# Kernel gradients of two output tiles per PSUM bank, written dense by ScalarE and permuted for the DRAM layout by GpSimd

## The chip, the cores and the metric

The kernel runs on one core of one Trainium2 chip. The metric is the device time of one execution in microseconds (us); a kernel is judged by the median of its runs. The core has five engines that run side by side, each through its own queue in a fixed order: TensorE (PE in the profile; its weight loads are PEld), VectorE (DVE), ScalarE (ACT), GpSimd (POOL) and SyncE (SP). Results of matmuls land in PSUM, which has banks of 512 fp32 columns; everything else on the chip is in SBUF, with 128 partitions.

## The reference

The reference is the forward pass and all gradients of one block, with L = 2048 positions, D = 576 channels, N = 128 states per channel and F = 4608 hidden units:

```python
xn = layernorm(x)
K  = einsum("dn,dnl,dn->dl", C, exp(dt*A*l), dt*B).real   # one kernel per channel
s  = irfft(rfft(xn) * rfft(K))[:L] + xn * Dskip           # long convolution
g  = silu((silu(xn @ w1) * (xn @ w3)) @ w2)               # gated FFN
out = x + s * g
# returned: out and the gradients of x, A, B, C (re, im), log_dt, Dskip, w1, w3, w2
```

What the change touches is the gradient of the convolution kernel, gK[d, l]: the correlation of the gradient of `s` with `xn`, for each channel. Two things are wanted of it downstream: gK itself and gK times the position l. Both are contracted with the state exponentials to give the gradients of A, B, C and log_dt.

## The kernel before

The program is built by a tile framework that schedules it: each piece of code gets a due time with `self.at(us)`, and the framework writes one fixed order of instructions per engine from those due times, with semaphore waits between engines. Nothing is reordered at run time. Independent work is mixed by choosing due times that overlap.

The stages, by the time in the profile: a prologue (layernorm, DFT matrices), the generation of K beside the first FFN matmuls, the forward convolution beside the second FFN matmul, then the backward part, which has two streams on the same engines:

- **FFN backward** (`phase6_group`, 18 groups of 256 hidden units). Per group: loads `w2r`, `h_n` and `gg_n` on GpSimd's queue (L1139, L1144, L1145), activations on ScalarE (L1149, L1151), matmuls into `ph` (L1172), ScalarE's copy to `gh` (L1175), VectorE's products (L1178), then weight gradients into `pgw` (L1200, L1218), which ScalarE copies to `gw` (L1204, L1221) and GpSimd's queue stores (L1205, L1222). The ring of `gw` has four buffers of each kind.
- **Convolution backward** (`ssm_bwd_conv`, `conv_bwd_quarter`, four quarters of 144 channels each). The sequence is cut into four blocks of 512, and the correlation is done by spectra of these blocks (DFT as matmul).

In one quarter, first the spectra `g` of the gradient are made (L564, copied out by ScalarE at L568). Then, for the blocks i = 3, 2, 1, 0 of gK, VectorE forms the spectrum Z as a sum of 4 - i complex products (`cmul_acc`, L601 to L610) and from it ZZ (L913 or L916, then L918). PE transforms ZZ back in four tiles of 128 positions x 144 channels (`idft_tile`, eight matmuls of 144 columns each, L582). This is one burst. Each tile has a PSUM bank of its own from a pool of three (`et_ps`). ScalarE empties it with four ACTIVATEs of 72 columns (L926, L927): for each half h of the channels one scaled by 1/512 and one scaled by the position (`lcol`). They write the order that DRAM is to have: in `gk_st` the tile's index t runs fastest, so that neighbouring elements of one ACTIVATE lie 32 elements apart in the buffer. After block 0 two DMAs on SyncE's queue store `gk_st` to `gK_dram` (L929). The second half of the quarter makes the gradient of `xn` in the same way, with VectorE adding each tile to `gx` (L947).

After the four quarters the parameter stage runs (`param_quarter`): it loads `gz` from `gK_dram` (L959, from 1317.9 us on), multiplies with the state exponentials on PE (L970) and reduces on VectorE (L977, L979), beside the last FFN groups. The last stage, `phase6_inputs`, makes the gradient of x (`px`, L1262) from the stored FFN gradients, which are loaded with transposing DMAs from SyncE's queue (L1123).

Of the kernel before, what the change touches and what calls it, by code (L numbers as in the profile page):

```python
# [10 lines left out]
ACT = mybir.ActivationFunctionType  # L11
# [3 lines left out]
BF16 = mybir.dt.bfloat16  # L15
I32 = mybir.dt.int32
P = 128
# [43 lines left out]
class K:  # L61
# [777 lines left out]
    def ssm_bwd_conv(self, T0, TQ, ps):  # L839
        nc, cfg = self.nc, self.cfg  # L840
        D, LT = cfg.D, cfg.LT
        self.gK_dram = self.dram.tile([4, P // 2, D // 64, 2, 2, 16 * LT], BF16, name="gK_dram")
        with self.tc.tile_pool(name="b_k", bufs=1, side="right") as kp, self.tc.tile_pool(name="b_z", bufs=2, side="right") as zp:
            self.at(T0)
            self.lcol = kp.tile([P, LT], FP32, name="lcol")
            nc.vector.tensor_scalar(out=self.lcol[:], in0=self.irow[:, 0:LT], scalar1=float(P),
                                    scalar2=self.pcol[:, 0:1], op0=ALU.mult, op1=ALU.add)
            nc.vector.tensor_scalar(out=self.lcol[:], in0=self.lcol[:], scalar1=1.0 / 512, scalar2=None, op0=ALU.mult)
            self.ones_col = kp.tile([P, 1], BF16, name="ones_col")
            nc.vector.memset(self.ones_col[:], 1.0)  # L850
            for g in range(4):
                self.conv_bwd_quarter(g, kp, zp, ps, T0 + g * TQ, TQ)

    def ssm_bwd_params(self, T0, TC, S_all, ps):
        cfg = self.cfg
# [7 lines left out]
            for g in range(4):  # L863
                self.param_quarter(g, gz, S_all, qp, ps, T0 + TC * g * D // 64, TC)

    def conv_bwd_quarter(self, g, kp, zp, ps, T0, TQ):
        nc, cfg = self.nc, self.cfg
        D, LT, KT, NB = cfg.D, cfg.LT, cfg.KT, cfg.NB
        W = D // 4
        cs = slice(g * W, (g + 1) * W)  # L870
        A2 = [None] * NB
        Az = [None] * NB
        fl = lambda t_: t_[:].rearrange("p q r k d -> p (q r) (k d)")
        self.at(T0)
        gs = kp.tile([P, LT, W], BF16, name="gs")
        nc.sync.dma_start(out=gs[:], in_=self.GS_dram[g])
        for b in range(NB):
            a3 = kp.tile([P, 3, KT, W], BF16, name=f"a3_{b}")
            nc.sync.dma_start(out=a3[:, 1], in_=self.UH_dram[g, b, :, 0])
            nc.sync.dma_start(out=a3[:, 0], in_=self.UH_dram[g, b, :, 1])  # L880
            A2[b], Az[b] = a3[:, None, 1:3], a3[:, None, 0]
            self.spectrum_variants(A2[b], Az[b])
        G = []
        for b in range(NB):
            self.at(T0 + TQ * 0.05 * b)
            G.append(kp.tile([P, 1, 2, KT, W], BF16, name=f"g_{b}"))
            self.dft_block(ps, lambda tt: gs[:, b * KT + tt, :], G[b])
        gds = ps.tile([P, 512], FP32, name="et_ps")
        for b in range(NB):
            prod = zp.tile([P, KT, W], BF16, name="gsxn")  # L890
            for tt in range(KT):
                t = b * KT + tt
                nc.vector.tensor_tensor(out=prod[:, tt, :].rearrange("p (h d) -> p h d", h=2),
                                        in0=gs[:, t, :].rearrange("p (h d) -> p h d", h=2),
                                        in1=self.nat4(self.xn_bf[:, t, :])[:, g], op=ALU.mult)
            for tt in range(KT):
                nc.tensor.matmul(gds[0:1, 0:W], lhsT=self.ones_col[:], rhs=prod[:, tt, :], start=(b == 0 and tt == 0),
                                 stop=(b == NB - 1 and tt == KT - 1))
        gds_sb = zp.tile([1, W], BF16, name="gds_sb")
        nc.scalar.copy(out=gds_sb[:], in_=gds[0:1, 0:W])  # L900
        with nc.allow_non_contiguous_dma(reason="small vector store"):
            nc.sync.dma_start(out=self.aps["out_9"].rearrange("(o h g d) -> o g h d", o=1, h=2, g=4)[:, g],
                              in_=gds_sb[:].rearrange("p (h d) -> p h d", h=2))
        st = kp.tile([P, D // 64, 2, 8, 2, LT], BF16, name="gk_st")
        nxt = None
        for i in range(NB - 1, -1, -1):
            self.at(T0 + TQ * (0.2 + 0.1 * (NB - 1 - i)))
            Z = zp.tile([P, 1, 2, KT, W], BF16, name="Z")
            for k, m in enumerate(range(i, NB)):
                self.cmul_acc(Z, A2[m - i], Az[m - i], G[m], zp, k == 0, True)  # L910
            ZZ = zp.tile([P, 1, 2, KT, W], BF16, name="ZZ")
            if nxt is not None:
                nc.vector.scalar_tensor_tensor(out=fl(ZZ), in0=fl(nxt), scalar=self.sgn[:, 0:1], in1=fl(Z), op0=ALU.mult,  # L913
                                               op1=ALU.add)
            else:
                nc.vector.tensor_copy(out=ZZ[:], in_=Z[:])  # L916
            nxt = Z
            nc.vector.tensor_scalar(out=ZZ[:, 0, :, 0, :], in0=ZZ[:, 0, :, 0, :], scalar1=self.hrow[:, 0:1], scalar2=None,  # L918
                                    op0=ALU.mult)
            for oc in range(KT):  # L920
                t = i * KT + oc
                pt = ps.tile([P, 512], FP32, name="et_ps")
                self.idft_tile(pt, ZZ, oc)
                for h in range(2):
                    pv = pt[:, h * W // 2:(h + 1) * W // 2].rearrange("p (c d) -> p c d", d=8)
                    nc.scalar.activation(out=st[:, :, 0, :, h, t], in_=pv, func=ACT.Copy, scale=1.0 / 512)  # L926
                    nc.scalar.activation(out=st[:, :, 1, :, h, t], in_=pv, func=ACT.Copy, scale=self.lcol[:, t:t + 1])  # L927
        for hf in range(2):
            nc.sync.dma_start(out=self.gK_dram[g, :, :, :, hf, :],  # L929
                              in_=st[64 * hf:64 * hf + 64].rearrange("p c k d h t -> p c k (d h t)"))  # L930
        for b in range(NB):
            a3 = kp.tile([P, 3, KT, W], BF16, name=f"a3_{b}")
            nc.sync.dma_start(out=a3[:], in_=self.KH_dram[g, b])
            A2[b], Az[b] = a3[:, None, 1:3], a3[:, None, 0]
        for j in range(NB):
            self.at(T0 + TQ * (0.6 + 0.1 * j))
            Z = zp.tile([P, 1, 2, KT, W], BF16, name="Z")
            for k, i in enumerate(range(NB - j)):
                self.cmul_acc(Z, A2[i], Az[i], G[i + j], zp, k == 0, True)
            gx = zp.tile([P, KT, W], FP32, name="gx")  # L940
            nc.vector.tensor_tensor(out=gx[:], in0=gs[:, j * KT:(j + 1) * KT, :],
                                    in1=self.dskip_row[:, None, cs].to_broadcast([P, KT, W]), op=ALU.mult)
            for oc in range(KT):
                t = j * KT + oc
                pt = ps.tile([P, 512], FP32, name="et_ps")
                self.idft_tile(pt, Z, oc)
                nc.vector.tensor_tensor(out=gx[:, oc, :], in0=pt[:, 0:W], in1=gx[:, oc, :], op=ALU.add)  # L947
            nc.scalar.dma_start(out=self.GXN_dram[:, j * KT:(j + 1) * KT, cs], in_=gx[:])
# [439 lines left out]
```

## Time and profile before

| | |
|---|---|
| median of 13 runs | 2046.72 us (2031.19 to 2065.65) |
| the profiled execution | 2057.42 us, of which the span is 2055.6 us |
| granted TensorE clock, mean | 0.948 |
| PE busy | 1770.4 us, 86% of the span |
| DVE busy | 1428.6 us, 69% |
| ACT busy | 992.4 us, 48% |
| POOL busy | 365.8 us, 18% |
| L926 and L927 in the window 850 to 1290 us | 79.7 and 82.4 us busy, 128 instructions each |
| first and last of them | 857.1 and 1273.3 us |

The span is the time from the first to the last instruction of the profile. "Busy" counts a stretch once, however many instructions of an engine overlap in it; instructions on ACT and DVE do overlap, since one starts before the last one's end. A line such as `L926 ACT ACTIVATE gk_st<-et_ps` names the source line, the engine, the operation, and what it writes and reads; the shapes are partitions x elements per partition. A line of the waits says who waited for whom, the total in us, how often, and the longest. In a timeline a bracket at the end gives the idle time of the engine before that instruction and what ended it.

### The profile page before, as it was taken

What the parts mean: (1) busy time and instruction counts of PE and PEld (TensorE: products, weight loads), DVE (VectorE), ACT (ScalarE), POOL (GpSimd) and SP (SyncE); (2) the same over time, 40 slices, a digit from 0 to 9 for tenths busy, and PEclk for the clock granted to TensorE, in tenths of its full rate; (3) what the DMA queues carried; (4) which work ended last, traced back from release to release, by engine and by line L of the source; (5) the groups of instructions that cost most, each with busy time, mean ns of one, the idle gap of its engine ahead of it and who ended that gap; (6) DMA issues with size and microseconds to landing.
All of it is one profiled execution on the core that took longest, in us unless ns stands there. A gap on an engine that the chain in (4) does not pass through costs nothing. (4 is left out here: it accounts for less than half of the span.)

```text
span 2055.6 us, 42197 instructions
## 1 busy us (share of the span) xinstructions
PE 1770.4 (86%) x17174; PEld 1296.6 (63%) x17174; DVE 1428.6 (69%) x2772; ACT 992.4 (48%) x1668; POOL 365.8 (18%) x540
## 2 busy tenths in 40 slices
PE   2889999999699995899888998898899839999891
PEld 1544444444488874788767777786788727777681
DVE  7538888888387723595964958676788725858567
ACT  2778888888445545766636556343364200000000
POOL 4003333333312102111111211221112100000000
PEclk9899999999899997999999999999999969999996
DMA  3588888896966568365653645798899599999980
GB/s 83 195 285 307 305 296 301 290 321 248 303 145 168 133 139 268 124 197 153 171 162 100 200 149 163 200 264 203 184 223 215 158 225 215 193 233 191 212 154 22
DMA packets 595505, 416.06 MB, mean 202 GB/s; under 512 B 404912, under 2 KB 537136, under 8 KB 590704
## 3 DMA queue, kind: packets, MB, share of 16 engines
q1 hardware_dynamic: 539632, 264.00, 53.8%
q0 software_dynamic: 30544, 120.94, 17.1%
q10 hardware_dynamic: 25136, 28.44, 5.3%
q8 instruction: 134, 2.20, 0.5%
q14 instruction: 59, 0.48, 0.1%
HBM read 133.01 MB, written 188.01 MB: 156 GB/s over the span
## 5 line engine op out<-in xcount | busy, mean ns | idle before, releaser
L719 PE MATMUL pgu<-wmB_w,xnT 128*128 128x512 bf16 x1152 | 282.4, 380 | 1.8 <-ACT E_k L392 1.4
L1262 PE MATMUL px<-wTB_w,guc 128*128 128x288 bf16 x1152 | 244.6, 293 | 26.3 <-DMA guc<-GU_dram 14.3
L1262 PE MATMUL px<-wTB_w,ggc 128*128 128x288 bf16 x1152 | 246.5, 293 | 21.7 <-DMA ggc<-GG_dram 12.0
L1218 PEld LDWEIGHTS <-xn_bf 128*128 128x128 bf16 x2304 | 227.3, 99 | 54.4 <-issue 25.2
L977 DVE TENSOR_TENSOR pr_q<-et_ps,pz 128x512 f32<-128x512 f32 x288 | 186.6, 681 | 93.5 <-PE et_ps L970 93.5
L1172 PE MATMUL ph<-w2T,goT 128*128 128x256 bf16 x1440 | 188.6, 282 | 7.9 <-ACT gh L1175 5.9
L719 PEld LDWEIGHTS <-xnT 128*128 128x128 bf16 x1152 | 103.2, 98 | 124.4 <-issue 19.5
L1279 ACT ACTIVATE t<-gx 128x576 f32<-128x576 f32 x16 | 10.9, 683 | 348.2 <-DVE gx L1265 304.2
L979 DVE TENSOR_REDUCE S_all<-pr_q 128x16 f32<-128x1024 f32 x144 | 174.0, 1212 | 0.5
L1200 PE MATMUL pgw<-go_o,h_n 128*128 128x288 bf16 x1152 | 158.8, 291 | 8.3 <-DVE h_n L1154 8.1
L1172 PEld LDWEIGHTS <-goT 128*128 128x128 bf16 x1440 | 141.7, 101 | 31.3 <-issue 7.6
L1221 ACT CAST gw<-pgw 128x256 bf16<-128x256 f32 x144 | 53.7, 379 | 219.3 <-PE pgw L1218 175.0
L1262 PEld LDWEIGHTS <-guc 128*128 128x128 bf16 x1152 | 114.5, 100 | 59.0 <-DMA guc<-GU_dram 15.9
L1218 PE MATMUL pgw<-gg_n,xn_bf 128*128 128x256 bf16 x1152 | 134.9, 279 | 17.7 <-ACT gw L1221 17.7
L784 PE MATMUL po<-w2g,hc 128*128 128x288 bf16 x1152 | 148.6, 286 | 1.7 <-DMA hc<-H_dram 1.7
L1262 PEld LDWEIGHTS <-ggc 128*128 128x128 bf16 x1152 | 114.0, 100 | 52.5 <-issue 11.4
L1200 PEld LDWEIGHTS <-h_n 128*128 128x128 bf16 x1152 | 113.1, 100 | 38.1 <-DVE h_n L1154 8.8
L1218 PE MATMUL pgw<-gu_n,xn_bf 128*128 128x256 bf16 x1152 | 132.2, 272 | 4.1 <-ACT gw L1221 2.0
L784 PEld LDWEIGHTS <-hc 128*128 128x128 bf16 x1152 | 111.3, 98 | 29.1 <-DMA hc<-H_dram 2.2
L722 ACT ACTIVATE s_t<-pgu 128x512 bf16<-128x512 f32 x144 | 87.4, 609 | 53.5 <-PE pgu L721 53.2
L1222 POOL DMA_DIRECT2D out_dram<-gw x144 | 77.6, 540 | 190.3 <-ACT gw L1221 186.1
L1175 ACT CAST gh<-ph 128x512 bf16<-128x512 f32 x144 | 83.3, 615 | 50.1 <-PE ph L1172 29.3
(305 smaller groups left out, 3724.9 us busy)
## 6 DMA issues: line engine op xcount, KB each, us to landing
GI_dram<-gu_t POOLq DMA_DIRECT2D x72, 512.0 KB, 5.7
H_dram<-h_t SPq DMA_DIRECT2D x72, 256.0 KB, 5.2
Q_dram<-q_k SPq DMA_DIRECT2D x36, 512.0 KB, 5.2
gg_n<-GI_dram POOLq DMA_DIRECT2D x18, 1024.0 KB, 5.6
h_n<-GI_dram POOLq DMA_DIRECT2D x18, 1024.0 KB, 8.7
GU_dram<-gu_n SPq DMA_DIRECT2D x36, 512.0 KB, 4.6
GG_dram<-gg_n SPq DMA_DIRECT2D x36, 512.0 KB, 7.1
E_dram<-E_k SPq DMA_DIRECT2D x18, 768.0 KB, 3.6
```

What stands on the lines that cost most here:

```text
L719: nc.tensor.matmul(pgu[:, j], lhsT=xnT[:, c, ts], rhs=wm[w][:, c, :], start=(c == 0), stop=False)
L722: nc.scalar.activation(out=s_t[:, :, q, :], in_=pgu[:, 0].rearrange("p (g f) -> p g f", g=ng), func=ACT.Silu)
L784: nc.tensor.matmul(pos[k][:, pi_, 0:pw], lhsT=hcs[k][:, fi, :], rhs=w2[fi][:, po:po + pw], start=(fi == 0), stop=(fi == FT - 1))
L977: nc.vector.tensor_tensor(out=pr[:, r], in0=T[r][:], in1=pz[:, s + r, h * 8:h * 8 + 8, :][:, :, None, :] .to_broadcast([P, 8, 2, AV]), op= ...
L979: nc.vector.tensor_reduce(out=S_all[:, 2 * s:2 * s + 2, d0:d0 + 8].rearrange("p k d -> p d k"), in_=pr[:].rearrange("p r d k a -> p d k r ...
L1172: nc.tensor.matmul(ph[j][:, k, :].rearrange("p (a f) -> p a f", f=P), lhsT=lw, rhs=rh, start=(n == 0), stop=(n == nfull))
L1175: nc.scalar.copy(out=gh[:, j], in_=ph[j][:])
L1200: nc.tensor.matmul(pgw[pi_][:, 0:pw], lhsT=hn[:, tt, fl * P:(fl + 1) * P], rhs=go_o[:, tt, po:po + pw], start=(tt == 0), stop=(tt == LT - 1))
L1218: nc.tensor.matmul(pw_[:, 0:FG], lhsT=self.xn_bf[:, tt, c * P:(c + 1) * P], rhs=nat[:, tt, :], start=(tt == 0), stop=(tt == LT - 1))
L1221: nc.scalar.copy(out=gw[:], in_=pw_[:, 0:FG])
L1222: nc.gpsimd.dma_start(out=aps[oname][c * P:(c + 1) * P, fb:fb + FG], in_=gw[:])
L1262: nc.tensor.matmul(px[pi_][:, 0:pw], lhsT=act[:, fi, :], rhs=wT[part][ai][:, f, po:po + pw], start=(fi == 0 and ai == 0), stop=(fi == FT - ...
```

## The change

The two tiles of a pair are transformed into one bank, side by side. ScalarE empties the pair with three ACTIVATEs that write dense rows of a new buffer `gk_sd` (two in rotation, one per block i): one of 288 columns for the scale 1/512, and one of 144 columns per tile for the position. When the four tiles of a block are in `gk_sd`, GpSimd copies them to `gk_st` in the order that DRAM is to have, with four copies of 288 elements per partition (9 x 8 x 4; one per scale k and half h); each writes runs of four elements and reads with a step of 288 elements. The two stores to `gK_dram` are as before and wait for GpSimd's copies now.

```diff
+                self.tc.tile_pool(name="b_s", bufs=2, side="right") as sp:
...
-            for oc in range(KT):
-                t = i * KT + oc
+            sd = sp.tile([P, KT, 2, W], BF16, name="gk_sd")
+            for o2 in range(0, KT, 2):
+                t = i * KT + o2
                 pt = ps.tile([P, 512], FP32, name="et_ps")
-                self.idft_tile(pt, ZZ, oc)
+                for j in range(2):
+                    self.idft_tile(pt[:, j * W:(j + 1) * W], ZZ, o2 + j)
+                nc.scalar.activation(out=sd[:, o2:o2 + 2, 0, :], in_=pt[:, 0:2 * W].rearrange("p (t d) -> p t d", t=2),
+                                     func=ACT.Copy, scale=1.0 / 512)
+                for j in range(2):
+                    nc.scalar.activation(out=sd[:, o2 + j, 1, :], in_=pt[:, j * W:(j + 1) * W], func=ACT.Copy,
+                                         scale=self.lcol[:, t + j:t + j + 1])
+            for k in range(2):
                 for h in range(2):
-                    pv = pt[:, h * W // 2:(h + 1) * W // 2].rearrange("p (c d) -> p c d", d=8)
-                    nc.scalar.activation(out=st[:, :, 0, :, h, t], in_=pv, func=ACT.Copy, scale=1.0 / 512)
-                    nc.scalar.activation(out=st[:, :, 1, :, h, t], in_=pv, func=ACT.Copy, scale=self.lcol[:, t:t + 1])
+                    nc.gpsimd.tensor_copy(out=st[:, :, k, :, h, i * KT:(i + 1) * KT],
+                                          in_=sd[:, :, k, h * W // 2:(h + 1) * W // 2].rearrange(
+                                              "p t (c d) -> p c d t", d=8))
```

Per quarter ScalarE goes from 64 ACTIVATEs of 72 columns to 24 (8 of 288 columns, 16 of 144), and GpSimd gains 16 copies. Matmuls and DMAs are the same in number and size.

More of the change, by code (lines that the diff above doesn't have):

```diff
@@ L842, in ssm_bwd_conv @@
         self.gK_dram = self.dram.tile([4, P // 2, D // 64, 2, 2, 16 * LT], BF16, name="gK_dram")
-        with self.tc.tile_pool(name="b_k", bufs=1, side="right") as kp, self.tc.tile_pool(name="b_z", bufs=2, side="right") as zp:
+        with self.tc.tile_pool(name="b_k", bufs=1, side="right") as kp, \
+                self.tc.tile_pool(name="b_z", bufs=2, side="right") as zp, \
+                self.tc.tile_pool(name="b_s", bufs=2, side="right") as sp:
             self.at(T0)
@@ L851, in ssm_bwd_conv @@
             for g in range(4):
-                self.conv_bwd_quarter(g, kp, zp, ps, T0 + g * TQ, TQ)
+                self.conv_bwd_quarter(g, kp, zp, sp, ps, T0 + g * TQ, TQ)
     def ssm_bwd_params(self, T0, TC, S_all, ps):
@@ L864, in ssm_bwd_params, with conv_bwd_quarter @@
                 self.param_quarter(g, gz, S_all, qp, ps, T0 + TC * g * D // 64, TC)
-    def conv_bwd_quarter(self, g, kp, zp, ps, T0, TQ):
+    def conv_bwd_quarter(self, g, kp, zp, sp, ps, T0, TQ):
         nc, cfg = self.nc, self.cfg
```

## Prediction

> **What bounds the kernel now.** I read the page first (span, busy shares), then the chain that ended last, then the waits and windows of the stretch that the diff touches. Times are of the profiled execution: 2057.42 us, of which the span is 2055.6. The 13 runs shown have a median of 2046.72, 0.5% lower. I work out a difference against the profiled execution and take it off the median.
>
> The page: TensorE (PE) is the fullest engine, and the changed work (L926, L927) lies between 857 and 1274 us. The chain, three pieces of it:
>
> ```profile
> 1623.29 10.64 PE pgw L1218 x96
> 1637.08 6.52 DMA out_dram<-gw
> 1643.67 4.87 SPq L1123
> ```
>
> The end is tied to the last FFN gradient group: its last gradient is stored at 1637, then SyncE issues transposed loads, then `px` runs to the end. PE takes its work in one written order. So what PE loses or gains between 857 and 1274 moves everything behind it by that much, as long as nothing else holds PE there. Next the waits of PE and VectorE (DVE) in that stretch (columns: total us, times, longest):
>
> ```profile
> PE et_ps L582 <- ACT gk_st L927: 22.4, 22, 3.2
> PE et_ps L582 <- DVE gx L947: 9.0, 3, 4.2
> PE ph L1172 <- ACT gh L1175: 5.3, 6, 1.3
> DVE gu_n L1178 <- ACT gh L1175: 40.1, 15, 5.4
> ```
>
> PE waits 22.4 us for a PSUM bank that ScalarE (ACT) has not yet emptied into `gk_st`. The wait for `gh` is partly the same thing: the `gh` copies are queued on ACT behind the `gk_st` burst. But DVE is nearly full in the same places. Windows around the four bursts (us of PE, PEld, DVE, ACT, POOL busy):
>
> ```profile
> 855.00:875.00 20.00, 15.38 (x147) 12.57 (x145) 16.50 (x29) 19.97 (x46) 0.56 (x1) 0.91 0.22 64
> 875.00:905.00 30.00, 27.00 (x282) 23.61 (x280) 28.78 (x51) 16.55 (x47) 8.09 (x15) 1.00 0.64 212
> 960.00:1013.00 53.00, 45.19 (x448) 37.54 (x447) 48.79 (x91) 36.00 (x97) 8.62 (x16) 0.97 0.42 123
> 1112.00:1160.00 48.00, 40.50 (x413) 35.05 (x411) 42.23 (x75) 32.62 (x88) 8.64 (x16) 0.96 0.51 157
> 1226.00:1275.00 49.00, 40.60 (x411) 34.92 (x410) 42.03 (x75) 31.85 (x88) 8.65 (x16) 0.97 0.42 132
> ```
>
> Over these 200 us PE is idle 31.3 (20-15.4, 30-27, 53-45.2, 48-40.5, 49-40.6), DVE 21.7. Both are late because of ACT, and DVE, which makes each ZZ, is the next limit.
>
> **The change, part by part.**
>
> *ACT.* A tile costs four scattered ACTIVATEs, 256 in all. They start 0.32 us apart:
>
> ```profile
> 861.26 0.80 ACT L926 ACTIVATE gk_st<-et_ps 128x72 bf16<-128x72 f32 x1
> 861.58 0.81 ACT L927 ACTIVATE gk_st<-et_ps,lcol 128x72 bf16<-128x72 f32 x1
> 960.28 0.62 ACT L568 CAST g<-et_ps 128x144 bf16<-128x144 f32 x3
> 974.63 0.70 ACT L1204 CAST gw<-pgw 128x288 bf16<-128x288 f32 x2 [0.52 <-PE pgw L1200]
> ```
>
> Two tiles are 8 x 0.32 = 2.56 us. After: one dense op of 288 columns (0.70 / 2 = 0.35) and two of 144 (0.62 / 3 = 0.21 each), 0.77 us. Over 32 pairs ACT sheds 32 x 1.79 = 57 us. PE needs about 0.06 us per matmul of 144 columns, 1.0 us for the 16 of a pair, so ACT keeps ahead with three banks: the 22.4 us wait goes. One price: reading starts after two tiles, not one, so 0.5 us later per burst, which a burst that is some 1.8 us x 2 shorter covers.
>
> *PE.* The built program has the same matmuls in nearly the same order; a few FFN matmuls that stood between two tiles of a pair now stand behind it. I put that at nothing, since they stay within the burst.
>
> *GpSimd (POOL).* 64 copies of 288 elements per partition, four per block row. No row shows this copy (it reads with a step of 576 bytes). The rows near it:
>
> ```profile
> L642 POOL COPY k<-k x16: 292/344/1129, 555.2 to 694.2; 1x144 bf16<-1x144 bf16 x16
> L477 POOL TENSOR_SCALAR pz_k<-pz_k x36: 1479/1488/1714, 150.9 to 509.5; 128x512 bf16<-128x512 bf16 x36
> ```
>
> Twice L642's undisturbed 0.29 is 0.58 us; L477's 2.9 ns an element gives 0.83; the whole of L477, 1.48, is my dear end. 64 copies are 37, 53 or 95 us; POOL is busy 8 us in each of the windows above. Where do they stand in its queue? In the built program each group of four is ahead of the next `gw` store, `w2r` and `h_n` loads. Laid on the old times, a burst of four ready at 862.4, 871.4, 884.3 and so on delays a store behind it by at most 2.7 us at 0.8 us a copy; `w2r` and `h_n` by 1 us. The `gw` ring is four deep, so I put that at nothing; at 1.48 the delay is about 5.5 us, a few of which could reach PE through `gw`. The `gK_dram` store on SyncE now waits for POOL instead of ACT: ACT ends some 3.6 us earlier and four copies take 2.3 to 3.3, so it is no later; the last one's reader starts at 1317.9, 43 us on.
>
> *The price on DVE.* The copies meet DVE ops that read two SBUF tensors. The trace shows what that does:
>
> ```profile
> 250.46 0.42 DVE L483 TENSOR_TENSOR t_k<-pz_k,nWiT 128x512 bf16<-128x512 bf16 x1
> 250.53 1.71 POOL L477 TENSOR_SCALAR pz_k<-pz_k 128x512 bf16<-128x512 bf16 x1 [2.96 <-DVE pz_k L475]
> 250.80 0.83 DVE L483 TENSOR_TENSOR t_k<-pz_k,WrT 128x512 bf16<-128x512 bf16 x1
> ```
>
> The second L483 takes 0.83 instead of its median of 0.417: POOL keeps it off for 0.41 us, a quarter of its own 1.71, or 0.81 ns per element; L642 cost a DVE op beside it 0.105 us for 144 elements, 0.73 ns. For 288 elements that is h = 0.23 us per copy as the low end; the high end is a copy that holds DVE throughout, 0.58 to 0.83. I take h = 0.35: nearest to L642's and L477's hold, half as much again because of the stepped read, which is my choice. [...]
>
> *The sum.* In each quarter 12 of 16 copies fall before DVE's last ZZ: 12h = 4.2 us. DVE also sheds its wait for `gh` there (3.50, 2.64, 2.22, 1.63 us). These and PE's waits are the gaps in brackets in the timeline, two of them here:
>
> ```profile
> 867.67 0.22 PE L582 MATMUL et_ps<-ZZ,dC 128*128 128x144 bf16 x1 [3.17 <-ACT gk_st L927]
> ...
> 872.34 0.69 DVE L1178 TENSOR_TENSOR gu_n<-gh,gu_n 128x1024 bf16<-128x1024 bf16 x1 [3.50 <-ACT gh L1175]
> ```
>
> The last burst of a quarter starts when both PE and ZZ are there:
> - Quarter 1: PE started it at 897.0 and sheds 5.75 us of waits on ACT before it (1.11, 3.17, 0.35, 0.54, 0.58), so 891.3; ZZ comes at 892.6 - 3.5 + 4.2 = 893.3. Start 3.5 earlier, and 1.9 of waits go inside or behind the burst: -5.4.
> - Quarter 2: ZZ 1004.1 - 2.64 + 4.2 = 1005.7 against 1004.3: +1.4, less 2.4 inside: -1.0.
> - Quarter 3: PE at 1147.8, ZZ at 1149.1 - 2.2 + 4.2 = 1151.1 against 1153.5: -2.4, and 1.8: -4.2.
> - Quarter 4: ZZ 1264.8 - 1.6 + 4.2 = 1267.4 against 1265.6: +1.8, less 3.1: -1.3.
> - Behind the bursts DVE sheds 10.8 us of `gh` waits; of PE's 9.0 us for `gx` I take 2.
>
> Together -14 us: 2043 against the profiled 2057.4, 2033 against the median. By h, the sum moves 48 us per us: h = 0.23 gives -20, 0.58 gives -3, 0.83 gives +9. What is late next is DVE's ZZ.
>
> **The rivals.**
> - *DVE is not the limit*: all of PE's 22.4, the 5.3 for `gh` and some 3 for `gw` go: -31, 2016. For it: DVE's own waits are ACT's doing. Against: ZZ stands within 2 us of PE's need in 11 of 16 bursts. Chance 0.12.
> - *The port eats the gain*: the copy holds DVE throughout, 0.58 to 0.83 us: -3 to +9, about 2047. For it: the stepped read. Against: the 0.41 of 1.71. Chance 0.25.
> - *Slower*: same mechanism, place and price, at L477's full 1.48 us of hold: 48 x (1.48 - 0.35) - 14 = +40, 2087. It turns to a loss at h = 0.64, and passes 0.5% at 0.86. Chance 0.13.
> - *It doesn't do what it says*: ACT is off PE's path, or the dense writes cost as much as the scattered. L568's 0.21 against 0.32 and the waits speak against: 2047. Chance 0.05.
>
> **The numbers.** Forecast 0.45, at 2033 (its own range 2027 to 2040). I take 2017 to 2057, which leaves out the slower case and the edge of the largest gain. A measurement tells 0.5%, 10 us, from no change. Faster by more: four fifths of the forecast's 0.45 (h under 0.43) and the 0.12: 0.48. Slower by more: the 0.13 and a little: 0.14. Within: 0.38.
>
> **What would show it.** Right: the `gk_st` wait of PE is near zero, ACT sheds over 50 us in the four windows, `gh` waits of DVE fall by over 10 us, and PE waits for ZZ grow from 2.1 us to 5 or 10. The hold is read from TENSOR_TENSORs that start beside a copy: under 0.45 us over the usual 0.75 for 1152 elements is right. Wrong: copies above 1 us with DVE ops stretched by as much; `gw`, `w2r` or `h_n` late behind POOL; or a stretch behind 1320 us that absorbs what was gained.

## The result, and the profile after

The kernel after the change takes **2078.79 us** (median of 11 runs, 2068.34 to 2082.35); the kernel before, measured beside it, 2045.59 us (48 runs). The ratio is **1.0167, 95% interval 1.0142 to 1.0192**: slower by 33 us, where the forecast was 2033 us and the range ended at 2057. Executions of one kernel differ by up to 2% (the kernel before: 2026.68 to 2066.54 us) and the profiled one of the kernel before is among its slower ones (2057.42 us), so times are compared by medians and ratios, and traces by stages and waits. From here on source lines are those of the changed kernel; behind the loop they are ten higher than before (L1218 is now L1228, L1221 is L1231), inside it two (L918 is L920).

The page of the profiled execution; the group's columns are busy us and mean ns, then the idle time before it:

```profile
span 2079.0 us, 42116 instructions
...
PE 1771.1 (85%) x17174; PEld 1299.5 (63%) x17174; DVE 1452.2 (70%) x2772; ACT 940.0 (45%) x1508; POOL 467.9 (23%) x604
...
L935 POOL COPY gk_st<-gk_sd 128x288 bf16<-128x288 bf16 x64 | 102.7, 1648 | 69.3 <-ACT gk_sd L928 66.2
```

ACT sheds 52 us (992.4 to 940.0), as foreseen. POOL gains 102, because a copy lasts 1.65 us on average. PE does hardly more than before (1771.1 us for 1770.4) and DVE 24 us more (1452.2 for 1428.6), so for PE the added time is mostly waiting. The waits of 850 to 1350 us (total, times, longest):

```profile
PE pgw L1228 <- ACT gw L1231: 38.7, 6, 13.3
...
DVE gu_n L1188 <- ACT gh L1185: 27.2, 9, 6.6
...
PE et_ps L582 <- DVE ZZ L920: 21.1, 6, 7.2
...
PE et_ps L582 <- DVE gx L957: 13.0, 4, 5.2
```

PE's 22.4 us for `gk_st` are gone, and DVE waits 15 us less for `gh`. In their place PE waits 38.7 us for `gw` (9.0 before, over 850 to 1320) and 21.1 us for ZZ (2.1 before). From the first ZZ matmul to the last Z matmul the convolution stage lasts 493.4 us, before 460.7: +32.7, as much as the medians differ by. (The two profiled executions differ by 23.4 us only; behind the stage the one after is 9 us shorter, 730 us against 739. That stretch lasts 721 to 746 us in the other traces with an unchanged parameter stage.) In the stage PE is idle for 82.9 instead of 54.1 us, and for the same number of matmuls it is busy for 410.8 instead of 406.8 us, with a granted clock of 0.93 instead of 0.97 there. So waits make up 29 of the 33 us; the other 4 go with the lower clock. The same windows as in the prediction (PE, PEld, DVE, ACT, POOL busy, then PE clock):

```profile
855.00:875.00 20.00, 16.46 (x168) 13.97 (x166) 20.00 (x28) 13.42 (x27) 8.53 (x9) 1.00 0.28 76
875.00:905.00 30.00, 23.47 (x194) 19.56 (x194) 29.04 (x49) 5.16 (x15) 19.81 (x17) 0.77 0.49 163
960.00:1013.00 53.00, 43.84 (x456) 37.33 (x454) 47.95 (x80) 26.26 (x59) 24.40 (x28) 0.95 0.50 143
```

In the second window DVE is full, ACT nearly idle, POOL twice as busy, and PE has 194 matmuls where it had 282, at a clock of 0.77 where it was 1.00. What happens there is read from three timelines. GpSimd's queue (start, duration; the copies' 13.30 us is four of them together):

```profile
880.60 13.30 POOL L935 COPY gk_st<-gk_sd 128x288 bf16<-128x288 bf16 x4 [2.82 <-ACT gk_sd L928]
893.85 2.14 POOL L1232 DMA_DIRECT2D out_dram<-gw  x4
896.44 1.07 POOL L1232 DMA_DIRECT2D out_dram<-gw  x2 [0.44 <-ACT gw L1231]
```

VectorE over the same time, the beginning and the end of the copies' 13 us:

```profile
880.58 0.74 DVE L607 TENSOR_TENSOR cm_t<-g,a 128x1152 bf16<-128x1152 bf16 x1
881.25 0.74 DVE L604 TENSOR_TENSOR cm_t<-a,g 128x1152 bf16<-128x1152 bf16 x1
881.91 0.44 DVE L609 TENSOR_TENSOR Z<-Z,cm_t 128x576 bf16<-128x576 bf16 x1
...
889.28 0.68 DVE L1163 TENSOR_TENSOR gg_n<-gg_n,h_n 128x1024 bf16<-128x1024 bf16 x1
889.88 1.82 DVE L915 SCALAR_TENSOR_TENSOR ZZ<-Z,sgn 128x1152 bf16<-128x1152 bf16 x1
891.62 1.15 DVE L1164 TENSOR_TENSOR h_n<-gu_n,h_n 128x1024 bf16<-128x1024 bf16 x1
892.70 0.69 DVE L920 TENSOR_SCALAR ZZ<-ZZ,hrow 128x288 bf16<-128x288 bf16 x1
893.31 1.15 DVE L1163 TENSOR_TENSOR gg_n<-gg_n,h_n 128x1024 bf16<-128x1024 bf16 x1
```

And ScalarE, then TensorE, right behind it:

```profile
895.77 0.37 ACT L1231 CAST gw<-pgw 128x256 bf16<-128x256 f32 x1 [8.10 <-DMA out_dram<-gw]
```

```profile
896.20 6.55 PE L1228 MATMUL pgw<-gg_n,xn_bf 128*128 128x256 bf16 x32 [5.44 <-ACT gw L1231]
```

Read them together. The first copy begins at 880.60 and does not end before 890.48: while DVE issues two-input operations back to back, each of its usual length, **the copy stands still for over 9 us** (0.66 us is what the last of the four takes). Then the four copies get through, one beside each of the last four DVE operations shown, and each of these is now longer: 1.82 instead of 1.42, 1.15 instead of 0.68, 0.69 instead of 0.29, 1.15 again, so 0.40 to 0.47 us per copy. Meanwhile the stores of `gw` stand behind the copies on GpSimd's queue. The four `gw` buffers are full, ACT waits 8.1 us for one, and PE 5.4 us for ACT. The first copy of six of the sixteen bursts lasted 4.1 to 10.2 us in this way; the longest burst of four took 13.6 us. The usual lengths, from a place without copies:

```profile
1009.50 1.42 DVE L915 SCALAR_TENSOR_TENSOR ZZ<-Z,sgn 128x1152 bf16<-128x1152 bf16 x1
1011.50 0.29 DVE L920 TENSOR_SCALAR ZZ<-ZZ,hrow 128x288 bf16<-128x288 bf16 x1
```

L920 reads one tensor (and one value per partition) and is stretched like the others (0.69 us for 0.29), so it is not only two-input operations that a copy keeps off.

In quarters 2 and 4 there is a longer way round. Here are the waits of SyncE, before and after, over 840 to 1400 us:

```profile
SPq L929 <- ACT gh L1175: 54.5, 4, 14.6
```

```profile
SPq L939 <- POOL gk_st L935: 80.8, 4, 21.3
```

SyncE's queue stands up to 21.3 us at the `gK_dram` store. The transposes behind it that empty `w2r` come late, so the next `w2r` load on GpSimd's queue waits, and the `gw` stores stand behind that:

```profile
1044.08 1.08 POOL L1149 DMA_DIRECT2D w2r<-in_B_w_dram  x2 [15.88 <-DMA w2T<-w2r]
1045.15 0.53 POOL L1155 DMA_DIRECT2D h_n<-GI_dram  x1
1045.67 0.57 POOL L1215 DMA_DIRECT2D out_dram<-gw  x1
1046.23 2.14 POOL L1232 DMA_DIRECT2D out_dram<-gw  x4
```

PE's longest wait, 13.26 us until 1055.2, ends when ACT gets a `gw` buffer back from these stores. (In the kernel before the same `w2r` load waits 10.2 us and is issued 14 us earlier, and PE waits 4.4 us there.)

### The profile page after: what moved, and what is told of

The parts are those of the page before. It is cut to its first block, busy times and chain, and to the rows that moved or that the text cites. A ratio compares the mean times of both kernels' runs of the same rounds, so it can differ in the third digit from the quotient of the medians.

```text
span 2079.0 us, 42116 instructions
## 1 busy us (share of the span) xinstructions
PE 1771.1 (85%) x17174; PEld 1299.5 (63%) x17174; DVE 1452.2 (70%) x2772; ACT 940.0 (45%) x1508; POOL 467.9 (23%) x604
## 5 line engine op out<-in xcount | busy, mean ns | idle before, releaser
L1228 PEld LDWEIGHTS <-xn_bf 128*128 128x128 bf16 x2304 | 231.3, 101 | 96.5 <-issue 62.8
L1228 PE MATMUL pgw<-gg_n,xn_bf 128*128 128x256 bf16 x1152 | 143.2, 288 | 53.9 <-ACT gw L1231 53.9
L1231 ACT CAST gw<-pgw 128x256 bf16<-128x256 f32 x144 | 53.2, 373 | 267.4 <-PE pgw L1228 183.8
L1228 PE MATMUL pgw<-gu_n,xn_bf 128*128 128x256 bf16 x1152 | 133.2, 274 | 5.1 <-DVE gu_n L1188 3.6
L935 POOL COPY gk_st<-gk_sd 128x288 bf16<-128x288 bf16 x64 | 102.7, 1648 | 69.3 <-ACT gk_sd L928 66.2
L728 POOL DMA_DIRECT2D GI_dram<-gu_t x72 | 68.5, 952 | 214.3 <-DVE gu_t L724 112.1
```

Source lines behind the costliest of these rows:

```text
L728: nc.gpsimd.dma_start(out=self.GI_dram[fb * ng:(fb + 1) * ng, :, :, i0:i0 + NT, :].rearrange("g p u t f -> p u g (t f)"), in_=gu_t[:].rear ...
L935: nc.gpsimd.tensor_copy(out=st[:, :, k, :, h, i * KT:(i + 1) * KT], in_=sd[:, :, k, h * W // 2:(h + 1) * W // 2].rearrange("p t (c d) -> p ...
L1228: nc.tensor.matmul(pw_[:, 0:FG], lhsT=self.xn_bf[:, tt, c * P:(c + 1) * P], rhs=nat[:, tt, :], start=(tt == 0), stop=(tt == LT - 1))
L1231: nc.scalar.copy(out=gw[:], in_=pw_[:, 0:FG])
```

## The experiments

**Theory.** ScalarE's share of the change is a gain. The copies lose it twice: they read SBUF beside a busy DVE, which delays the ZZ on PE's path; and they are held up themselves, so that everything behind them on GpSimd's and SyncE's queue is late and `gw` stops PE. **Rivals.** The dense writes or the shared banks are themselves no gain; or the copies cost because they are more work on GpSimd's queue, whatever they read; or their step of 576 bytes makes them dear.

Four sets of runs of the kernel before were taken. Their medians: 2050.94 us beside ScalarE's part alone, the ring, the dense read and the copies on VectorE; 2050.47 beside the work without reads, the store on GpSimd's queue and both kernels with runs of 8; 2049.83 beside the control and the kernels with runs of 2 and 4; 2056.01 beside the last run. Ratios are to the kernel before of the same set.

### ScalarE's part alone

```diff
-            sd = sp.tile([P, KT, 2, W], BF16, name="gk_sd")
+            sd = sv[:, i * KT:(i + 1) * KT]     # sv: a dense view of gk_st
...
-                    nc.gpsimd.tensor_copy(out=st[...], in_=sd[...])
```

> ScalarE's dense writes and the paired banks as in the changed kernel, but no copies on GpSimd: the dense rows go straight into the buffer that is stored, so the order in DRAM and with it the gradients of A, B, C and log_dt are not computed. Both theories of the loss (queue: the copies hold up the stores behind them on GpSimd's queue; port: the copies slow VectorE) say that everything lost lies in the copies: then PE's waits for gk_st, gw and ZZ are all small, and the time is 14 to 31 us below the kernel before, 2015 to 2032. The rival that the paired tiles or the new order cost the time says 2060 or more.

Measured: 2026.41 us, ratio **0.9884 (0.9856 to 0.9912)**. The stage lasts 432.9 us. PE's waits of 850 to 1350 us:

```profile
PE et_ps L582 <- DVE gx L953: 8.9, 3, 3.8
PE pgw L1224 <- ACT gw L1227: 6.9, 5, 2.9
PE et_ps L582 <- DVE ZZ L921: 6.7, 4, 3.1
```

So the first rival falls: the dense writes into paired banks gain 24 us, and all of the loss, and this gain on top, comes with the copies.

### A ring of its own for gw

```diff
+            self.gwp13 = ffn.enter_context(pool(name="e_gw13", bufs=10))
...
-                gw = gwp.tile([P, FG], BF16, name="gw13")
+                gw = self.gwp13.tile([P, FG], BF16, name="gw13")
```

> The changed kernel with ten buffers instead of four for the 256-column weight gradients gw, so that ScalarE and PE need not wait while their stores stand behind the copies. The queue theory says: PE's wait for gw falls from 38.7 us in the convolution stage to under 12, and the time by 25 to 30 us, to about 2050. The port theory alone says that the gw wait only hid the wait for ZZ: under 10 us come off, 2069 or more, and PE's wait for ZZ grows from 21 us by what gw loses.

Measured: 2060.15 us, ratio **1.0016 (0.9977 to 1.0055)**. Against the changed kernel that is 0.0151 of 2050 us, 31 us back (with some 10 of uncertainty). The copies are as before; PE's waits are now led by ZZ, and none is for `gw`:

```profile
PE et_ps L582 <- DVE ZZ L920: 23.6, 6, 9.1
PE et_ps L582 <- DVE gx L957: 11.7, 6, 8.1
PE et_ps L582 <- DVE Z L609: 10.0, 2, 6.2
```

What is left against the kernel without copies is 0.0132, 27 us. The profiled execution took 2036.4 us, far from the median, so its whole length says little; the stage in it lasts 459.1 us, 34.3 less than in the changed kernel and 26.2 more than without copies, which agrees with the ratios. In the trace DVE's operations in the stage sum to 416.6 us, without copies to 389.3: 27 us, or 0.43 us for each of 64 copies. In the trace of the changed kernel itself they sum to 413.4, which is 0.38 us a copy; a copy that meets no DVE operation, as three of the four from 907.23 on, costs DVE nothing.

### The control: the same ring on the kernel before

The edit is the one above, on the kernel before.

> The kernel before with ten buffers of its own for the gw tiles, as the ring experiment gave the changed kernel: the control. Theory (the ring took back a queue that the copies had made): before had 9.0 us of PE waits on gw in the convolution stage, so it gains at most those, 0 to 9 us, and the 31 us that the ring gave the changed kernel are the copies'. Rival (the ring is worth the same anywhere): about -30 us, 2020.

Measured: 2040.08 us, ratio **0.9951 (0.9916 to 0.9986)**, a gain of 10 us (3 to 17), a little over what I had allowed it. So not quite all of the 31 us need be the copies' doing: between 21, if the ring's own gain comes on top, and 31, if the copies were merely added to the same queue. With the ring on both sides the change costs 0.0065, 13 us.

### Work on GpSimd without reads

```diff
-                    nc.gpsimd.tensor_copy(out=st[...], in_=sd[...])
+                    nc.gpsimd.memset(sd[:, :, k, h * W // 2:(h + 1) * W // 2], 0.0)
```

This is the kernel without copies, with 64 memsets of the same 288 elements that wait for the same ScalarE writes and stand in the same place of GpSimd's queue. It overwrites gK with zeros, so it leaves out the gradients of A, B, C and log_dt.

> ScalarE's dense writes into the stored buffer, as without the permutation, and in the place of each copy on GpSimd a memset of the same 288 elements, which waits for ScalarE as the copy does but reads nothing (gK is overwritten with zeros, so the gradients of A, B, C and log_dt are not computed). If the loss comes from reads of SBUF that GpSimd and VectorE keep each other from, a memset takes under 0.5 us however busy VectorE is, no VectorE op is stretched, and the time is that without the permutation, about 2028. The rival that it is the waiting for ScalarE in GpSimd's queue, or any work there, says that 15 us or more of the loss stay: 2045 to 2075.

Measured: 2027.02 us, ratio **0.9884 (0.9818 to 0.995)**, as without copies.

```profile
L936 POOL MEMSET gk_st<- x64: 327/332/347, 862.0 to 1245.7; 128x288 bf16 x64
```

```profile
L935 POOL COPY gk_st<-gk_sd x64: 658/1139/10209, 860.2 to 1300.7; 128x288 bf16<-128x288 bf16 x64
```

(Above the memset, below the copy of the changed kernel: min/median/max ns.) The memset is never held up, DVE loses nothing (389.9 us), and four instructions more per burst on GpSimd's queue cost nothing. That settles it against the second rival: it is not the mere work in that queue. A memset differs from a copy in two ways, though: it reads nothing, and it writes rows, not the scattered order. That a copy which reads and writes one dense row is held up too is shown by one line of the kernel before (`k<-k`, up to 1.13 us for 0.29, quoted further below), so the reading is the likely cause, and no run separates it from the scattered write. What each engine lost to the other differs widely: DVE 0.40 to 0.47 us to a copy that lasts 0.67 us alone, and the copy at 880.60 over 9 us, in which it ran beside nineteen DVE operations.

### Reading dense, writing scattered

```diff
-                    nc.gpsimd.tensor_copy(out=st[:, :, k, :, h, i * KT:(i + 1) * KT],
+                    nc.gpsimd.tensor_copy(out=st[:, :, k, :, h, i * KT:(i + 1) * KT].rearrange("p c d t -> p t c d"),
                                           in_=sd[:, :, k, h * W // 2:(h + 1) * W // 2].rearrange(
-                                              "p t (c d) -> p c d t", d=8))
+                                              "p t (c d) -> p t c d", d=8))
```

> The same copies on GpSimd with the loops turned round: they read runs of 72 elements and write single elements with a step of 64 bytes. If the stepped read makes the copy hold the port, a copy alone takes under 0.5 us instead of 0.67, a VectorE op of 1152 elements beside one is stretched by 0.25 us instead of 0.5, and PE's wait for ZZ falls by some 8 us; the copies that wait 4 to 10 us for VectorE stay, and so does the wait for gw: about 2068. If a copy costs by its elements, nothing moves: 2079.

Measured: 2094.21 us, ratio **1.0225 (1.0174 to 1.0276)**: slower still.

```profile
L935 POOL COPY gk_st<-gk_sd x64: 1449/1722/10654, 860.8 to 1315.9; 128x288 bf16<-128x288 bf16 x64
```

With single elements written 64 bytes apart a copy follows the other every 1.25 us at the quickest, with runs of four written and a step of 576 bytes read every 0.61 us. I had expected 2068 or 2079. The first copies are held up as long as before (10.7 us), although they read dense, so the stepped read is not what holds them up. DVE's sum is 429.7 us, 40 more than without copies or 0.63 us a copy, not the 0.25 expected: the hold grew with the longer copy. What the stepped read costs by itself stays open, since the writes changed with it; the third rival falls for the hold-up alone.

### The copies on VectorE

```diff
-                    nc.gpsimd.tensor_copy(out=st[:, :, k, :, h, i * KT:(i + 1) * KT],
+                    nc.vector.tensor_copy(out=st[:, :, k, :, h, i * KT:(i + 1) * KT],
```

> The 64 copies on VectorE instead of GpSimd. [...] The queue theory says that the gw wait goes back to 9 us, so that the time is that of the prediction's sum with h = 0.36, 14 us below the kernel before: 2032. The port theory alone expects little better than the changed kernel, since VectorE loses about as much: 2065 to 2075.

Measured: 2057.89 us, ratio **1.0013 (0.9977 to 1.0049)**.

```profile
L935 DVE COPY gk_st<-gk_sd x64: 617/633/649, 862.4 to 1276.3; 128x288 bf16<-128x288 bf16 x64
```

```profile
PE et_ps L582 <- DVE ZZ L920: 22.7, 7, 7.2
```

A copy takes 0.55 us of DVE (the distance between two of them), 35 us for 64; I had reckoned with 0.36, which no run shows. The time lies between the two expected (2032; 2065 to 2075). PE's wait for `gw` is down from 38.7 to 3.0 us, as the queue theory says. Without that queue held up this kernel is as slow as the one with the ring: to do a copy on DVE, or to be kept off by it for 0.43 us, comes to nearly the same.

### The gK store on GpSimd's own queue

```diff
-            nc.sync.dma_start(out=self.gK_dram[g, :, :, :, hf, :],
+            nc.gpsimd.dma_start(out=self.gK_dram[g, :, :, :, hf, :],
```

> The changed kernel with the two stores of gk_st per quarter on GpSimd's queue, behind the copies, instead of SyncE's, where they waited 81 us for the copies with the transposes of w2T behind them. If the second and fourth quarter's long waits for gw (13.3 and 9.6 us) come round by SyncE (store waits, transposes of w2T late, w2r waits for them on GpSimd, gw stores behind w2r), they shrink by 15 us or more together, and those of the first and third (5.4 and 7.5) stay: about 2062. If the copies alone hold the stores up, nothing moves: 2079.

Measured: 2080.52 us, ratio **1.0189 (1.0119 to 1.0259)**; I had expected a gain that shows. PE's waits for `gw`:

```profile
PE pgw L1228 <- ACT gw L1231: 33.3, 5, 9.0
```

SyncE no longer waits for the copies (80.8 us in the changed kernel), and the two waits of the long way round fall from 13.3 to 6.7 us and from 9.6 to 7.5. The waits of quarters 1 and 3 grow by 1 to 1.5 us each. The stage lasts 482.9 instead of 493.4 us in the trace (it starts 2.2 us later and ends 8.3 earlier); the time does not show it, and its interval is too wide (14 us either way) to rule it out. So the detour over SyncE is a part of the queue's price, by the trace some 10 us, and the smaller one: most comes from the stores right behind the copies.

### No copies at all: another order in DRAM

If the stored order keeps R neighbouring channels together, ScalarE can write it from PSUM in two ACTIVATEs of 144 columns per tile, in runs of R elements, and nothing needs permuting. The price goes to the parameter stage, where PE then reads `gz` with a step of R elements. These kernels compute everything. For R = 8:

```diff
-                z = gkp.tile([P, 2, 2, 2, 16, LT], BF16, name=f"gz{i}")
+                z = gkp.tile([P, 2, 2, 2, 2, LT, 8], BF16, name=f"gz{i}")
...
-                for h in range(2):
-                    pv = pt[:, h * W // 2:(h + 1) * W // 2].rearrange("p (c d) -> p c d", d=8)
-                    nc.scalar.activation(out=st[:, :, 0, :, h, t], in_=pv, func=ACT.Copy, scale=1.0 / 512)
-                    nc.scalar.activation(out=st[:, :, 1, :, h, t], in_=pv, func=ACT.Copy, scale=self.lcol[:, t:t + 1])
+                pv = pt[:, 0:W].rearrange("p (h c d) -> p h c d", h=2, d=8)
+                for k, sc in enumerate((1.0 / 512, self.lcol[:, t:t + 1])):
+                    nc.scalar.activation(out=st[:, :, k, :, t, :].rearrange("p c h d -> p h c d"), in_=pv, func=ACT.Copy,
+                                         scale=sc)
...
-                                         rhs=gK[:, r, :, :, dl, :].rearrange("p k f t -> p (k f) t"),
+                                         rhs=gK[:, r, :, :, h, :, dd].rearrange("p k f t -> p (k f) t"),
```

> A version without copies: one tile per bank as before, and ScalarE writes the DRAM order itself, but in an order whose fastest index is eight channels and not the tile, so that each ACTIVATE takes all 144 columns and writes runs of 8 elements (two ACTIVATEs a tile instead of four). TensorE reads these with a step of 16 bytes in the parameter stage (1152 matmuls of 64 columns). If ScalarE's time goes by runs or instructions, an ACTIVATE starts 0.2 us after the one before, a burst takes ScalarE 1.7 us instead of 5.25, and PE's wait for gk_st is near zero: 20 to 25 us below the kernel before, as without the permutation at all, 2022 to 2030. The rival is that the stepped read on TensorE or 16-byte runs on ScalarE cost what was gained: no change, 2050.

The second kernel of this kind also puts two tiles in a bank, as the change does:

> The same, with two tiles in one bank as in the changed kernel, four ACTIVATEs of 144 columns a bank. If pairing is worth anything by itself, PE waits less for banks than with one tile a bank, and the time is some 5 us lower; if pairing was never what helped, the two are alike within 5 us.

Measured: 2084.7 us, ratio **1.0177 (1.0135 to 1.0219)**, and paired 2084.57, **1.0184 (1.0139 to 1.0229)**. The convolution stage is 29.6 us shorter than before. But the matmuls of the parameter stage, with a median of 193 ns in the kernel before and a start every 29 ns, go to 294 ns and 116 ns:

```profile
L970 PE MATMUL et_ps<-gz,qT x1152: 273/294/302, 1301.2 to 2010.2; 128*128 128x64 bf16 x192
```

1152 of them by 0.087 us are 100 us of PE, more than was gained; in the trace the stretch behind the convolution stage grows by 55 us. Pairing tiles showed no worth by itself: the two stages last 431.1 and 431.7 us.

With R = 2 and R = 4 (the tile `gz` is then `[P, 2, 2, 2, 2, 8 // R, LT, R]`, the read `gK[:, r, :, :, h, dd // R, :, dd % R]`, and the store is split by scale and half):

> The stored order keeps pairs of channels together, so ScalarE writes it straight from the bank in two instructions of 144 columns per tile (runs of 2 elements, 4 bytes), nothing is copied, and the parameter stage reads with a step of 4 bytes in place of 2. The whole gradient is computed. Theory (the loss of the change is the reads of the copies on GpSimd beside VectorE; ScalarE's share alone gains): the convolution stage loses the same 25 to 30 us as in the kernel without copies if two such instructions take under 0.55 us together, and the matmuls of the parameter stage stay near 190 ns, since with runs of 8 (step 16 bytes) they went from 193 to 294: time about 2022 to 2035. Rival (any step in what TensorE reads costs in full): these matmuls take 250 ns and more, and the time is 2060 or above.

> As the kernel with runs of 2, with runs of 4 channels: ScalarE writes runs of 8 bytes, TensorE reads in the parameter stage with a step of 8 bytes. The whole gradient is computed. Theory (cost of the step grows with its bytes, 0.029 us of spacing at 2 bytes, 0.116 at 16): if it doubles with each doubling from some point, 0.058 us at 8 bytes, the parameter stage loses up to 1152 x 0.03 = 33 us of TensorE time, part of it in its waits; the convolution stage gains 25 to 30: time 2022 to 2055. Rival (any step costs in full): 2080, as with runs of 8.

Measured: R = 2 **2026.66 us, ratio 0.9882 (0.984 to 0.9924)**; R = 4 2031.49 us, 0.9892 (0.9844 to 0.994). First the matmuls with R = 2, then with R = 4, then ScalarE's writes with R = 2:

```profile
L970 PE MATMUL et_ps<-gz,qT x1152: 189/192/261, 1304.1 to 1946.8; 128*128 128x64 bf16 x192
```

```profile
L970 PE MATMUL et_ps<-gz,qT x1152: 214/238/257, 1302.7 to 1960.9; 128*128 128x64 bf16 x192
```

```profile
L926 ACT ACTIVATE gk_st<-et_ps x64: 264/298/346, 859.4 to 1246.5; 128x144 bf16<-128x144 f32 x64
L926 ACT ACTIVATE gk_st<-et_ps,lcol x64: 362/382/439, 859.5 to 1246.7; 128x144 bf16<-128x144 f32 x64
```

Runs of two are enough for ScalarE: in a burst a tile follows the other every 0.43 us (the first two begin at 859.38 and 859.81), where four scattered ACTIVATEs 0.32 us apart took 1.28, and all these writes together keep ACT busy for 32.6 instead of 84.1 us. PE reads every second element as fast as dense ones, with a start every 29 ns; with R = 4 it is every 60 ns, 36 us of PE in all, and the intervals of the two times overlap. The stage lasts 433.5 us, as without copies. This version beats both kernels and computes the whole gradient. The last run gave it the ring as well:

> Runs of 2 channels written straight by ScalarE (ratio 0.988 alone) and ten buffers for the gw tiles (0.995 alone on the kernel before). If the two remove different waits, the parts add: about -24 - 10 = -34 us, ratio 0.983. If the ring only relieves what the slower ScalarE writes had held up, nothing is left for it (PE waits on gw are 4.2 us with runs of 2): ratio 0.986 to 0.989.

Measured: 2019.42 us, ratio **0.9851 (0.9812 to 0.9889)**. The lowest of all, by 1.5% against before; whether the ring adds to runs of two cannot be told (the intervals overlap).

## Why the prediction was wrong

It expected -14 us: some -31 from ScalarE and PE's waits, +17 from the hold on DVE, nothing from the queues. The runs give -24, +27 and +31. These are steps from one kernel to the next (without copies, with copies and ring, with copies), so they add up to the measured 33 to 34 us by construction; the stage lengths of the traces, -28, +26 and +34, show the same three steps.

- **ScalarE: right.** 52 us shed on the page (57 said), the `gk_st` wait gone, 15 us less of DVE's waits for `gh` (over 10 said). Alone it gained 24 us (18 to 30); the rival with no limit by DVE said 31.
- **The hold on DVE: right mechanism, size nearly right, effect too small.** h was taken as 0.35 us, half as much again as the two rows gave because the copy reads with a step, a choice that no run shows by itself; over all copies it is 0.38 in the changed kernel and 0.43 with the ring, and the four operations above show 0.40 to 0.47. By the 48 us per us of h that is 18 to 21 us, not 17; all that is left with the ring is 27 (with some 10 of uncertainty), and some of that may be other waits behind the copies. ZZ comes later than foreseen: PE waits 21.1 us for it, not 5 to 10. A likely reason, not shown by a run of its own: the copies get in when DVE's chain reaches ZZ (four of the six hold-ups ended beside L915), so that three of the four holds fall on L915, L920 and the operation between them, for which PE waits. With the hold alone the change would have come out at the kernel before, as the version with the ring did, or some 13 us above it if the ring's own gain is taken off. (In the sum of quarter 1 a start 3.5 us earlier should be 3.7 by its own times, which changes nothing.)
- **The failed step: "The `gw` ring is four deep, so I put that at nothing".** It rested on copies of 0.8 us and a delay of at most 2.7 us behind a burst. Measured: bursts of up to 13.6 us, 38.7 us of PE waits on `gw`, and 21 to 31 us of the time. The prediction asked only how long a copy keeps DVE off and never how long DVE keeps a copy off. The row for that was in its own quotation: `k<-k` on GpSimd with 292/344/1129 ns. It took the minimum and left the maximum unread. Three of the sixteen last 1.13 us. The timeline around one of them, in the kernel before, shows where that comes from:

```profile
636.45 0.45 DVE L610 TENSOR_TENSOR V<-V,cm_t 128x576 bf16<-128x576 bf16 x1
636.60 1.13 POOL L642 COPY k<-k 1x144 bf16<-1x144 bf16 x1 [2.35 <-DVE k L641]
636.82 0.75 DVE L607 TENSOR_TENSOR cm_t<-cu,k 128x1152 bf16<-128x1152 bf16 x1
637.76 0.76 DVE L604 TENSOR_TENSOR cm_t<-k,cu 128x1152 bf16<-128x1152 bf16 x1 [0.19 <-POOL k L642]
```

A copy of 0.29 us lasts 1.13, until the second of two DVE operations at their usual length is over; here DVE then had to wait for it. With a DVE that is full (28.78 of 30 us in the window 875 to 905) and waits for nothing, such a copy could be held far longer (10.2 us at the longest, as it turned out); this row and the windows together were the warning, though not a price.

- **"So it is no later" for the store on SyncE: wrong**, 21.3 us of wait at the longest (14.6 before), for the same reason. Moving the store took 7 us off what had been PE's longest wait, and nothing measurable off the time.
- **The rivals.** "Slower" said 2087 and is near the time, but by another way: it needed h above 0.64 us, and h was 0.38 to 0.43. Its end was right by luck, its mechanism not. "The port eats the gain" gave nearly the time of the version with the ring, with an h that was not reached. The step that the prediction listed as a sign of error, `gw` and `w2r` late behind POOL, is the one that came.
- **The copy itself: about right** where DVE leaves it alone, 0.67 us for 0.58 to 0.83 said.

What stays open: why ten of the sixteen bursts were not held up beside the same kind of DVE operations, why a held-up copy gets in where it does (four times beside L915, once beside L1188, once in a pause of DVE), whether the read alone does it, what it is that the two engines keep each other from (the "port" of the rival and of the expectations is a guess that no run shows), and how the 21 to 31 us of the queue split between copies and ring.

## What to carry to other kernels

Before work is moved to GpSimd beside a full VectorE, ask in both directions who is kept waiting, read the maximum of the nearest row as well as its minimum, and then ask what else stands in that queue: here the `gw` stores left GpSimd's queue only when 13.3 us of copies were through. A permutation that no engine has time for may be made cheap at both ends instead: here runs of two elements cut ScalarE's cost to 0.4 of what it was (84.1 to 32.6 us) and left TensorE's reads as they were (a matmul's median is 192 ns for 193).

## What the runs showed of the hardware

- A GpSimd copy from SBUF to SBUF that takes 0.67 us alone took up to 10.2 us beside back-to-back two-input DVE operations; a memset in the same place took 0.33 to 0.35 us at all times.
- Where copy and DVE operation did overlap, the operation mostly took 0.40 to 0.49 us longer, a one-tensor TENSOR_SCALAR included (0.69 us for 0.29).
- TensorE's 64-column matmul (bf16, moving operand from SBUF) starts every 29 ns with a step of 2 or 4 bytes in what it reads, every 60 ns with 8 and every 116 ns with 16. One of them lasts 193, 192, 238 and 294 ns in the median with steps of 2, 4, 8 and 16 bytes.
- A GpSimd copy of 288 elements follows the one before it after 1.25 us at the quickest when it writes single elements 64 bytes apart (the shortest lasts 1.45 us), after 0.61 when it writes runs of four and reads with a step of 576 bytes (0.66); the latter copy on VectorE after 0.55 (0.62).
